# Later V copies for pairs 4 to 7, and K, Q and V loads ahead of FFN weights, in a fused attention and FFN kernel

## The chip, the cores and the metric

The kernel runs on one core of one Trainium2 chip, in one launch. The metric is the device time in microseconds, as the median of several runs; lower is better. A profile is one execution, recorded instruction by instruction, with times counted from the start of its span. The engines are TensorE (PE, with its weight loads as PEld), VectorE (DVE), ScalarE (ACT), GpSimd (POOL) and SyncE (SP); POOL and SP also issue DMAs.

## The reference

Attention with pooled queries over 8 batches of 8 heads, 1152 positions of 64 features, and then a multiplicative FFN on the 4608 rows that come out:

```python
q_pool = q.reshape(B, H, S // 2, 2, D).mean(axis=3)       # 1152 -> 576 queries
scores = 1/sqrt(D) * q_pool @ k.transpose(0, 1, 3, 2)
attn = softmax(scores)
x = (attn @ v).transpose(0, 2, 1, 3).reshape(B * 576, 512)
a = x @ w1;  b = x @ w2                                   # 512 -> 1024
out = ((a * b) @ w3) @ w_out                              # 1024 -> 1024 -> 512
```

Inputs and output are float32; the kernel computes in float16 with float32 accumulation.

## The kernel before

**Pairs.** Two heads form a pair; there are 32 pairs (`NP`), each with 9 key blocks of 128 by 576 queries, 5184 score columns. Scores of consecutive pairs are strung together and cut into chunks of 512 columns. `scores(c)` computes a chunk for both heads on TensorE (line 292) into a PSUM buffer "psc", of which there are three; `expo(c)` takes the exponential on ScalarE into the ring `er` (line 302). `attend` (line 317) multiplies 128 queries by 128 keys of `er` with V; 45 such matmuls make one head, 90 a pair. They accumulate in "po", a single PSUM buffer, so the first matmul of a head waits until `normalize` of the head before (lines 330 and 334, VectorE) has read it.

**Steps.** The main loop has 108 steps (`it`, counted from 0) of three chunks. Each step emits its scores and exponentials, then preparation of later pairs, then a number of PV matmuls from the table `PVS`, around one or two groups of other TensorE work. A group "F" uses the single PSUM buffer "ff", a group "X" one of the three "psc". Groups are, early on, transposes of w3 (line 383) and products T = w3 w_out (line 395), then the FFN's first products "pa" and "pb" (line 411) and its rows "pp" (line 429). Each group's result is copied out by VectorE. With `brief`, where the next group is a transpose, 8 of the step's PV matmuls are emitted ahead of it. Every engine runs its instructions in the order in which they are emitted. After the loop a tail runs the rest of the FFN. In the profile step 12's scores start at 41.97 us, step 13's at 44.67, step 14's at 53.07, step 27's at 94.15, step 28's at 97.25.

**Preparation.** Pairs 1 to 7 are pooled and staged by VectorE (`prep_stage`, lines 122 and 165), transposed by TensorE (`prep_groups`, lines 257 and 169) and copied to `qT` and `kT` by VectorE (lines 263, 264 and 271). From pair 8 on two pairs at a time go another way (`prep_dma`): POOL pools q (line 122) and stages keys (line 142), SP's transposing DMAs make kT and qT (lines 145 and 148), and `settled` (line 152) makes POOL wait for kT before it issues the loads of two later pairs (`load_two`). SP's queue also carries the transposing DMAs of finished outputs (lines 342 and 345) and the stores of the result (line 450).

**V.** A load on POOL's queue brings V of a pair, cast to float16, into one of four staging buffers (`vst`, line 96). `copy_v` (line 135) copies it on VectorE into one of four buffers `vts[P % 4]`, which carry the column for the sum of the softmax. In the loop, `copied` counts these copies. Copies of pairs 1 to 3 are emitted at the end of a step, behind everything else; copies from pair 4 on after the step's scores and preparation, ahead of its PV matmuls and groups: pair 4's in step 12, 5's in step 15, 6's in 19, 7's in 22, 8's in 24. Pair 4 is first used by PV in step 17, pair 5 in 19, pair 6 in 24, pair 7 in 27.

**Loads.** All loads but three at the start go through POOL's queue in the order of emission. `more_loads` adds to it after staging: n = 2 in step 1, n = 3 in step 4, n = 4 in step 8, n = 5 (nothing) in step 11. `load_ffn(h)` loads half of the columns of w1 and w2, 512 KB written each (line 363). Pairs 8 and 9 are loaded by `load` in steps 16 and 19.

Of the kernel before, what the change touches and what calls it, by code (L numbers as in the profile page):

```python
# [23 lines left out]
def kernel(  # L24
# [18 lines left out]
    NP = B * H // 2  # L43
    SCL = 16.0
    NPE = 8
# [31 lines left out]
    def load_q(P):  # L77
        b, h0 = P // 4, 2 * (P % 4)
        if P % 2 == 0 or P == 1:
            qst[P // 2] = stage.tile([128, 2, 18, D], FP16, tag="qst", bufs=2, name="qst")  # L80
        o = 64 * (P % 2)
        nc.gpsimd.dma_start(
            out=qst[P // 2][o:o + 64].rearrange("p u t d -> p u (t d)"),
            in_=q[b, h0:h0 + 2].rearrange("u (p t) d -> p u (t d)", t=18))

    def load_k(P):
        b, h0 = P // 4, 2 * (P % 4)
        kst[P] = stage.tile([128, 2, NJ, D], FP16, tag="kst", name="kst")
        nc.gpsimd.dma_start(  # L89
            out=kst[P].rearrange("p u j d -> p u (j d)"),  # L90
            in_=k[b, h0:h0 + 2].rearrange("u (p j) d -> p u (j d)", j=NJ))

    def load_v(P):
        b, h0 = P // 4, 2 * (P % 4)
        vst[P] = stage.tile([128, 2, NJ, D], FP16, tag="vst", name="vst")
        nc.gpsimd.dma_start(  # L96
            out=vst[P].rearrange("p u j d -> p u (j d)"),
            in_=v[b, h0:h0 + 2].rearrange("u (p j) d -> p u (j d)", j=NJ))

    def load(P):  # L100
        if P < NP:
            load_k(P)
            load_q(P)
            load_v(P)

    def load_two(P):
        load_q(P)
        load_q(P + 1)
        load_v(P)
        load_v(P + 1)  # L110
        load_k(P)
        load_k(P + 1)
# [21 lines left out]
    def copy_v(P):  # L134
        nc.vector.tensor_copy(out=vts[P % 4][:, :, :, 0:D], in_=vst.pop(P))
# [15 lines left out]
    def settled(P):  # L151
        nc.gpsimd.tensor_copy(out=seen, in_=kT[P][0:1, 0, 0:1])
# [9 lines left out]
    def prep_stage(P):  # L162

        pool_q(P)
        nc.vector.tensor_copy(out=new_kc(P).rearrange("p j u d -> p u j d"), in_=kst.pop(P))
# [24 lines left out]
    def spin(n):  # L190
        t = psum.tile([128, 512], FP32, tag="ff", bufs=1, name="spin")
        for _ in range(n):
            nc.tensor.matmul(t[:, 0:128], hot, hot, start=True, stop=True)
# [55 lines left out]
    def prep_groups(P):  # L249

        pp, o = P // 2, 64 * (P % 2)
        new_kq(P)

        def few(t, n):
            if n == 0:
                for c in range(NJ):
                    nc.tensor.transpose(t[:, 128 + 64 * c:192 + 64 * c],
                                        qps[pp][o:o + 64, c].rearrange("p u d -> p (u d)"),
                                        ident[o:o + 64, o:o + 64])
                keys(P, t, range(8, 9))  # L260

        def few_end(t):
            nc.vector.tensor_copy(out=qT[P], in_=t[:, 128:704].rearrange("p (c f) -> p c f", f=64))
            nc.vector.tensor_copy(out=kT[P][:, 8], in_=t[:, 0:128])

        def many(t, n):
            if n == 0:
                keys(P, t, range(0, 8))

        def many_end(t):  # L270
            nc.vector.tensor_copy(out=kT[P][:, 0:8].rearrange("p j f -> p (j f)"), in_=t)  # L271
            del kcs[P]

        return [("t2", FP16, 1, few, few_end), ("t1", FP16, 1, many, many_end)]
# [5 lines left out]
    def scores(c):  # L280
        t = psum.tile([128, 2, CH], FP32, tag="psc", bufs=3, name="psc")
        psc[c] = t
        g = c * CH
        while g < (c + 1) * CH:
            J = g // SQ
            P, j = divmod(J, NJ)
            f0 = g - J * SQ
            ln = min(SQ - f0, (c + 1) * CH - g)
            o = g - c * CH
            for u in range(2):  # L290
                s = slice(64 * u, 64 * u + 64)
                nc.tensor.matmul(t[:, u, o:o + ln].rearrange("p (c f) -> p c f", f=64), kT[P][s, j, :],  # L292
                                 qT[P][s, f0 // 64:(f0 + ln) // 64], start=True, stop=True)
            g += ln

    def expo(c):
        r = (c * CH) % RING
        g = (c - RING // CH + 1) * CH
        if g > 0:
            Pg, Jg = divmod((g - 1) // SQ, NJ)  # L300
            assert nb >= 90 * Pg + 45 + 5 * Jg + 5
        nc.scalar.activation(out=er[:, :, r:r + CH], in_=psc.pop(c), func=AF.Exp,  # L302
                             bias=0.0, scale=SCALE)
# [18 lines left out]
    def ready(n, chunks):  # L322
        P, m = divmod(n, 90)
        j, i = divmod(m % 45, 5)
        return (P * NJ + j) * SQ + min(128 * i + 128, SQ) <= chunks * CH
# [26 lines left out]
    def load_w3(c0, n):  # L352
        if c0 % 4 == 0:
            w3h.append(ffp.tile([128, 4, dff], FP16, tag="g", name="w3h"))
        o = c0 % 4
        nc.gpsimd.dma_start(  # L356
            out=w3h[c0 // 4][:, o:o + n],
            in_=moe_w3.rearrange("(c p) f -> p c f", p=128)[:, c0:c0 + n])

    def load_ffn(h):  # L360
        cols = slice(512 * h, 512 * h + 512)
        for dst, src in ((w1sb, moe_w1), (w2sb, moe_w2)):
            nc.gpsimd.dma_start(
                out=dst[:, :, cols],
                in_=src.rearrange("(c p) f -> p c f", p=128)[:, :, cols])
# [124 lines left out]
    loaded, staged, prepped, copied = 8, 1, 1, 1  # L490

    def more_loads(n):
        if n == 2:
            load_k(4)
            load_q(4)
            load_v(3)
            load_w3(4, 2)
            load_w3(6, 2)
            load_k(5)
            load_q(5)  # L500
            load_v(4)
            load_ffn(0)
        elif n == 3:
            load_k(6)
            load_q(6)
            load_v(5)
            load_ffn(1)
            load_v(6)
        elif n == 4:
            load(7)  # L510
    rest = prep_first()

    n_units = NT // 512
# [37 lines left out]
    def first_it(P):  # L551
        return P * PAIR // (CH * BURST)
# [21 lines left out]
    for it in range(NIT):  # L574
        at = it * BURST * CH / PAIR
        while early and it >= early[0][0]:
            queue.append(early.pop(0)[1])
        while next_unit < EARLY:
            last_b = (512 * (next_unit + 1) - 1) // SQ
            if it < 3 or reached[it - 2] < 360 * (last_b + 1):  # L580
                break
            gens.append(ffn_groups(next_unit))
            next_unit += 1
        for w in range(BURST):
            if it == 0 and w == 2:
                rest()
            if it in (1, 2):
                spin(4)
            scores(BURST * it + w)
            expo(BURST * it + w)  # L590
        if 5 <= staged < NPE and it >= first_it(staged) - 3:
            prep_stage(staged)
            staged += 1
        while 8 <= loaded < NPE + 2 and at >= loaded - 3.4:
            load(loaded)
            loaded += 1
        urgent = False
        if prepped < NPE:
            if it >= first_it(prepped) - (1 if prepped < 5 else 2):
                queue[0:0] = prep_groups(prepped)  # L600
                prepped += 1
                urgent = True
        elif prepped < NP and at >= prepped - 1.95:
            prep_dma(prepped)
            if loaded < NP:
                settled(prepped)
                load_two(loaded)
                loaded += 2
            prepped += 2
        if 4 <= copied < NP and at >= copied - (1.1 if copied >= NPE else 0.6):  # L610
            copy_v(copied)
            copied += 1
        n = PVS[it]
        left = 45 - nb % 45
        brief = bool(queue) and queue[0][2] == 1
        a = left if left < n else 8 if brief and it > 8 and 8 < n < 40 and 8 < left else 0
        assert nb + n <= NPV and ready(nb + n - 1, BURST * it)
        pv(a)
        if head():
            group("F")  # L620
        if head() and (n < 40 or urgent or it < 17):
            group("X")
        pv(n - a)
        if staged < 5 and it >= first_it(staged) - 2:
            prep_stage(staged)
            staged += 1
            more_loads(staged)
        if copied < 4 and at >= copied + 0.25:
            copy_v(copied)
            copied += 1  # L630
        reached.append(nb)
# [43 lines left out]
```

## Time and profile before

| | us |
|---|---|
| median of 5 runs | 424.78 (422.96 to 425.67) |
| profiled execution, its own time | 422.75 |
| its span, first to last instruction | 421.0 |
| TensorE busy | 406.9 (97%) |
| ScalarE busy | 326.8 (78%), nearly all exponentials of 1028 ns |
| VectorE busy | 198.6 (47%) |
| mean granted TensorE clock | 0.996 |
| V copies (line 135) | 32, median 452 ns |
| loads of V, K and Q | 288 KB written each, 8.9, 11.0 and 6.2 us from issue to landing (medians) |

A line of the timeline reads: start in us, length in us, engine, line of the kernel, operation, what it writes and reads, shapes, how many instructions were merged, and in brackets the idle time of the engine just before and what ended it. "PEclk" is the granted clock of TensorE in tenths of full speed. "DMA to landing" counts from the issue of a transfer to its arrival. A busy TensorE is not the same as one at its peak, since the ends of matmuls are modelled.

### The profile page before, as it was taken

How to read it: one execution, taken by the hardware profiler on the slowest of the kernel's cores; microseconds unless marked ns; L12 is line 12 of the kernel's file. 1: busy time of each engine (PE TensorE's matmuls, PEld its weight loads, DVE VectorE, ACT ScalarE, POOL GpSimd, SP SyncE). 2: the span in 40 equal slices, each digit the busy share in tenths (PEclk: the TensorE clock that was granted, in tenths of full speed). 3: DMA queues.
4: the chain of work that ended last, by engine and by line, in shares of the span. 5: the costliest groups of instructions: out<-in, count | busy, mean ns of one | idle time of the engine just before them, and what ended most of it. 6: DMA issues, size and time to landing. Idle time of an engine off the chain costs nothing.

```text
span 421.0 us, 12708 instructions
## 1 busy us (share of the span) xinstructions
PE 406.9 (97%) x5507; PEld 271.7 (65%) x5507; DVE 198.6 (47%) x407; ACT 326.8 (78%) x357; POOL 121.1 (29%) x161
## 2 busy tenths in 40 slices
PE   7899699999999999999999999999999999999996
PEld 5677477766685668665775686667765876544443
DVE  2446546454555553555445534545445444613140
ACT  5999589989888889989888889898888889133332
POOL 6443331343434343434261523234151000000000
PEclk9999899999999999999999999999999999999999
DMA  8999999498989899999999979979997131050404
GB/s 193 202 196 206 199 203 192 79 161 144 167 164 193 120 176 172 205 133 177 176 200 137 145 131 173 168 116 191 171 167 135 44 76 30 14 115 2 100 2 100
DMA packets 95801, 59.76 MB, mean 142 GB/s; under 512 B 65152, under 2 KB 86144, under 8 KB 95744
## 3 DMA queue, kind: packets, MB, share of 16 engines
q0 software_dynamic: 26928, 32.97, 49.2%
q1 hardware_dynamic: 68656, 25.84, 34.8%
q8 instruction: 43, 0.70, 0.7%
q10 hardware_dynamic: 160, 0.13, 0.1%
q14 instruction: 14, 0.11, 0.1%
HBM read 67.11 MB, written 9.44 MB: 182 GB/s over the span
## 4 chain that ended last, share of the span: by engine, by line
PE 84%; DMA 10%; ACT 2%; POOL 1%; issue 1%; DVE 0%; SPq 0%; ACTq 0%
PE po L317 19%; PE psc L292 18%; PE pa L411 15%; PE pb L411 15%; PE pp L429 15%; DMA vst<-in_v_dram 4%; DMA w3h<-in_moe_w_dram 3%; DMA kst<-in_k_dram 3%; PE pT L395 2%; ACT er L302 2%; DMA out_dram<-osb 1%; DMA er<-in_k_dram 1%; PE w3t L383 0%; POOL xT L371 0%; POOL w3h L356 0%
## 5 line engine op out<-in xcount | busy, mean ns | idle before, releaser
L302 ACT ACTIVATE er<-psc 128x1024 f16<-128x1024 f32 x324 | 307.4, 1028 | 44.7 <-PE psc L292 44.6
L317 PEld LDWEIGHTS <-er 128*128 128x128 f16 x2880 | 103.6, 97 | 22.7 <-issue 5.9
L317 PE MATMUL po<-vt,er 128*128 128x65 f16 x2880 | 110.9, 193 | 0.1
L292 PE MATMUL psc<-qT,kT 64*128 64x512 f16 (+7 forms) x1152 | 95.2, 286 | 6.8 <-DVE kT L271 3.6
L423 DVE TENSOR_TENSOR gT<-pb,asb 128x512 f16<-128x512 f32 x72 | 49.8, 692 | 56.0 <-PE pb L411 55.3
L411 PE MATMUL pa<-xT,w1sb 128*128 128x512 f16 x288 | 74.2, 380 | 0.0
L411 PE MATMUL pb<-xT,w2sb 128*128 128x512 f16 x288 | 74.1, 380 | 0.0
L429 PE MATMUL pp<-T,gT 128*128 128x256 f16 (+1 forms) x488 | 67.9, 292 | 0.0
L292 PEld LDWEIGHTS <-kT 64*128 64x128 f16 x1152 | 45.5, 94 | 30.4 <-issue 6.9
L421 DVE COPY asb<-pa 128x512 f32<-128x512 f32 x56 | 38.7, 692 | 40.5 <-PE pa L411 39.4
L429 PEld LDWEIGHTS <-gT 128*128 128x128 f16 x488 | 45.6, 98 | 18.5 <-issue 3.7
L411 PEld LDWEIGHTS <-w2sb 128*128 128x128 f16 x288 | 26.4, 98 | 32.7 <-issue 3.9
L411 PEld LDWEIGHTS <-w1sb 128*128 128x128 f16 x288 | 25.1, 98 | 30.1 <-issue 6.0
L122 POOL TENSOR_TENSOR qp<-qst 128x1152 f16<-128x1152 f16 x12 | 28.3, 2356 | 44.2 <-DMA qst<-in_q_dram 34.1
L441 DVE TENSOR_SCALAR osb<-pp 128x256 f32<-128x256 f32 x49 | 20.8, 425 | 36.8 <-PE pp L429 30.5
L330 DVE RECIPROCAL rz<-po 128x5 f32<-128x5 f32 x64 | 12.4, 194 | 48.1 <-PE po L317 47.7
L334 DVE TENSOR_TENSOR xn<-po,rz 128x320 f16<-128x320 f32 x64 | 31.5, 492 | 2.5 <-DVE rz L330 0.3
L142 POOL COPY kc<-kst 128x576 int32<-128x576 int32 x24 | 16.0, 669 | 48.2 <-DMA kst<-in_k_dram 48.2
L96 POOL DMA_DIRECT2D vst<-in_v_dram x32 | 23.4, 737 | 13.7 <-DMA w3h<-in_moe_w_dram 5.7
L438 ACT ACTIVATE osb<-pp 128x512 f32<-128x512 f32 (+1 forms) x12 | 7.0, 579 | 24.0 <-PE pp L429 20.4
L89 POOL DMA_DIRECT2D kst<-in_k_dram x31 | 22.4, 731 | 7.0 <-DVE rz L330 2.0
L419 ACT COPY asb<-pa 128x512 f32<-128x512 f32 x16 | 9.4, 587 | 16.5 <-PE pa L411 16.5
(42 smaller groups left out, 152.3 us busy)
## 6 DMA issues: line engine op xcount, KB each, us to landing
vst<-in_v_dram POOLq DMA_DIRECT2D x32, 288.0 KB, 8.9
out_dram<-osb SPq DMA_DIRECT2D x70, 128.0 KB, 2.4
kst<-in_k_dram POOLq DMA_DIRECT2D x31, 288.0 KB, 11.0
qst<-in_q_dram POOLq DMA_DIRECT2D x31, 288.0 KB, 6.2
w3h<-in_moe_w_dram POOLq DMA_DIRECT2D x3, 512.0 KB, 14.6
xT<-in_moe_w_out_dram POOLq DMA_DIRECT2D x4, 256.0 KB, 10.7
w1sb<-in_moe_w_dram POOLq DMA_DIRECT2D x2, 512.0 KB, 14.9
w2sb<-in_moe_w_dram POOLq DMA_DIRECT2D x2, 512.0 KB, 16.1
```

What stands on the lines that cost most here:

```text
L89: nc.gpsimd.dma_start(out=kst[P].rearrange("p u j d -> p u (j d)"), in_=k[b, h0:h0 + 2].rearrange("u (p j) d -> p u (j d)", j=NJ))
L96: nc.gpsimd.dma_start(out=vst[P].rearrange("p u j d -> p u (j d)"), in_=v[b, h0:h0 + 2].rearrange("u (p j) d -> p u (j d)", j=NJ))
L122: eng.tensor_tensor(out=qps[pp][r].rearrange("p c u d -> p u c d"), in0=src[:, :, :, 0, :], in1=src[:, :, :, 1, :], op=ALU.add)
L292: nc.tensor.matmul(t[:, u, o:o + ln].rearrange("p (c f) -> p c f", f=64), kT[P][s, j, :], qT[P][s, f0 // 64:(f0 + ln) // 64], start=True, ...
L302: nc.scalar.activation(out=er[:, :, r:r + CH], in_=psc.pop(c), func=AF.Exp, bias=0.0, scale=SCALE)
L317: nc.tensor.matmul(po[P, u][:, VW * x:VW * x + D + 1], er[:, u, r:r + 128], vts[P % 4][:, u, j, 0:D + 1], start=(m == 0), stop=(m == 44), ...
L334: nc.vector.tensor_tensor(out=xn[:, P % 2, :, u, :], in0=acc[:, :, 0:D], in1=rz.to_broadcast([128, 5, D]), op=ALU.mult)
L411: nc.tensor.matmul(p, w[:, mc, ft * 128:ft * 128 + 128], xT[:, mc, t0:t0 + 512], start=(mc == 0), stop=(mc == NC - 1))
L421: nc.vector.tensor_copy(out=asb[ft], in_=p)
L423: nc.vector.tensor_mul(out=gT[:, ft, :], in0=p, in1=asb.pop(ft))
L429: nc.tensor.matmul(p[:, 0:n], gT[:, ft, 128 * i:128 * i + 128], T16[:, ft, n * s:n * s + n], start=(ft == 0), stop=(ft == NF - 1))
L441: nc.vector.tensor_scalar_mul(out=osb, in0=p[:, 0:n], scalar1=1.0 / (SCL * SCL))
```

## The change

Four things differ.

- The V copies of pairs 4 to 7 are emitted at the end of a step: pair 4's in step 15 (was 12), 5's in step 17 (was 15), 6's in step 21 (was 19), 7's in step 24 (was 22). Pair 8's copy, still ahead of its step's PV matmuls, comes in step 25 (was 24), since it waits for its turn behind pair 7's. Later copies stay where they are.
- POOL's load queue behind v4 (V of pair 4) was: ffn(0), k6, q6, v5, ffn(1), v6, k7, q7, v7. It is now: k6, q6, v5, ffn(0), k7, q7, v6, ffn(1), v7. Loads of pairs 8 and later follow as before.
- The loads of pair 7 are emitted one by one instead of by `load(7)`.
- The `brief` split is left out where a step starts exactly at the start of a head (`left` is 45). On TensorE this changes two steps, 13 and 19: the first 8 PV matmuls of the head move behind the w3 transposes and the T product that they stood ahead of.

No instruction is added or removed on any engine.

```diff
@@ more_loads
             load_k(5)
             load_q(5)
             load_v(4)
-            load_ffn(0)
         elif n == 3:
             load_k(6)
             load_q(6)
             load_v(5)
+            load_ffn(0)
+        elif n == 4:
+            load_k(7)
+            load_q(7)
+            load_v(6)
             load_ffn(1)
-            load_v(6)
-        elif n == 4:
-            load(7)
+            load_v(7)
@@ the main loop
-        if 4 <= copied < NP and at >= copied - (1.1 if copied >= NPE else 0.6):
+        if NPE <= copied < NP and at >= copied - 1.1:
             copy_v(copied)
             copied += 1
         n = PVS[it]
         left = 45 - nb % 45
         brief = bool(queue) and queue[0][2] == 1
-        a = left if left < n else 8 if brief and it > 8 and 8 < n < 40 and 8 < left else 0
+        a = left if left < n else 8 if brief and it > 8 and 8 < n < 40 and 8 < left < 45 else 0
...
-        if copied < 4 and at >= copied + 0.25:
+        if copied < NPE and at >= copied + (0.25 if copied < 5 else 0):
             copy_v(copied)
             copied += 1
```

Here `at` is the step's place counted in pairs (it x 1536 / 5184), and `NPE` is 8.

## The prediction

> **What bounds the kernel now.** I began with the page's busy shares and clock row: they say which engine the end hangs on.
>
> ```profile
> span 421.0 us, 12708 instructions
> ...
> PE 406.9 (97%) x5507; PEld 271.7 (65%) x5507; DVE 198.6 (47%) x407; ACT 326.8 (78%) x357; POOL 121.1 (29%) x161
> ...
> PEclk9999899999999999999999999999999999999999
> ```
>
> TensorE is the bound: 97% busy, and from 80 us to the tail its stretches are full (30.00 of 30.00 us in 90 to 120, 80.00 of 80.00 in 120 to 200). So a pause of TensorE removed early is worth its length at the end, unless a later wait takes it back. The one slice with a reduced clock is the fifth, 42 to 53 us. So I asked for the waits between 36 and 60 us (total, times, longest):
>
> ```profile
> ACT er L302 <- PE psc L292: 7.0, 6, 3.4
> DVE vt L135 <- DMA vst<-in_v_dram: 4.9, 2, 4.0
> ...
> PE psc L292 <- DVE kT L271: 3.5, 1, 3.5
> ```
>
> VectorE waits 4.0 us for a V load, TensorE 3.5 us for a copy of keys by VectorE, ScalarE 3.4 us for scores. The timeline of 42 to 53 us (start, us) shows that this is one event:
>
> ```profile
> 43.07 0.43 PE L257 MATMUL t<-ident,qp 64*128 64x64 f16 x9
> ...
> 45.36 0.28 PE L292 MATMUL psc<-qT,kT 64*128 64x256 f16 x2 [0.29 <-ACT er L302]
> ...
> 47.49 0.46 DVE L135 COPY vt<-vst 128x1152 f16<-128x1152 f16 x1 [4.00 <-DMA vst<-in_v_dram]
> 47.87 0.45 DVE L263 COPY qT<-t 128x576 f16<-128x576 f16 x1
> ...
> 48.37 0.68 DVE L271 COPY kT<-t 128x1024 f16<-128x1024 f16 x1
> ...
> 49.10 0.82 PE L292 MATMUL psc<-qT,kT 64*128 64x256 f16 x6 [3.46 <-DVE kT L271]
> ...
> 49.60 1.94 ACT L302 ACTIVATE er<-psc 128x1024 f16<-128x1024 f32 x2 [3.37 <-PE psc L292]
> ```
>
> The copy of V of pair 4 (step 12) stands on VectorE ahead of the copies of qT and kT of pair 4. TensorE had those transposes done by 44.1, but VectorE stood until 47.49, and the scores of pair 4 (in step 13) until 49.10. Then the clock, by windows (columns end in granted clock, DMA share, GB/s):
>
> ```profile
> 48.50:49.00 0.50, 0.00 (x0) 0.00 (x0) 0.50 (x2) 0.00 (x0) 0.20 (x1) 0.84 1.28 211
> ...
> 50.00:51.00 1.00, 1.00 (x15) 1.00 (x14) 0.92 (x2) 1.00 (x2) 0.70 (x1) 0.50 1.23 205
> ...
> 52.00:52.50 0.50, 0.50 (x5) 0.42 (x4) 0.06 (x1) 0.00 (x0) 0.00 (x0) 0.75 1.24 213
> ```
>
> After the pause the clock is half, from about 48.85 to 52.25 us.
>
> **Part 1: the V copy of pair 4 moves behind step 15's work.** What goes: 3.46 us of idle TensorE, and the half clock. TensorE works 49.10 to 52.25, 3.15 us at half rate, so up to 1.57 us lost. By rows: weight transposes and the first product after them take 50.29 to 52.55, 2.26 us, against 57.02 to 58.35, 1.33 us, for the same 16 at full clock; 0.93 lost there, and with the six score matmuls and eight PV matmuls before them, and those after, 1.2 to 1.6. I take 1.5. Sum 3.46 + 1.5 = 5.0 us (4.6 to 5.3).
>
> Can ScalarE follow? It is the tighter engine in this stretch (10.00 of 10.00 us in 10 to 20). Its last exponential before the pause ends at 46.22; before its next long run at 53.57 it idles 3.37 + 2.03 = 5.40 us, so it can give up 5.0. Built forward: L263 at about 43.7, kT copied by 44.9, scores of step 13 done at 45.9, the two groups to 47.2, 22 PV matmuls to 48.0; step 14's first exponential starts near 48.3 instead of 53.57. ScalarE bounds steps 13 to 15, and the gain is 5.2 by its row, 5.0 by TensorE's; I keep 5.0.
>
> What is late next? On VectorE, step 13's pooling of q of pair 5 follows at 45.5 and now meets its load: q5 was issued at 29.09 and took 17.2 us, so 46.3. A new wait of 0.8 us. Queued behind it are the key copy, w3T and T16 copies (0.45 + 0.69 + 0.42 us), done near 48.4. Who waits: the third score chunk of step 14, which takes the PSUM buffer of the T16 copy and is wanted at 48.5; and the transposes of pair 5, not wanted before 49.1. Hidden; if q5 were a microsecond later, up to 1 us of step 14 would show.
>
> The copy itself (0.45 us) runs at the end of step 15, near 54.3, with v4 landed since 47.5 (32.56 + 14.9); pair 4's PV starts in step 17, at 64.23 before, 59 now. Hidden by 4 us.
>
> **Part 2: V copies of 5, 6, 7, and of 8 one step later.** Each is 0.45 us. Copy 5 goes behind step 17's normalisation, into 0.46 us that VectorE sits idle before L263 at 66.82; 6 and 7 behind steps 21 and 24, where the idle is 1 us or more; 8 follows 7 in step 25 and just fits (copies would end 89.3 on the old clock, next item 89.39). Uses come two to four steps later. The 0.87 us that copy 5 waited for v5 at 57.51 also goes; no TensorE wait hung on it. Worth 0, from -0.3 to +0.2. The staging slots come free later (v8 needs copy 4, v9 copy 5, v11 copy 7), but POOL issues v8 at 60.49, v9 at 66.44 and v11 after 90.98, so always after the new copy times (54.8, 61.7, 83.7).
>
> **Part 3: the split of 8 PV matmuls at a head's start.** It alters TensorE's order in two steps, 13 and 19: two groups run before the head instead of behind 8 matmuls of it. In 19 the second group's PSUM buffer comes free at 70.52 and is now asked for at 70.29: 0.25 us idle, against ScalarE bounding the next scores (they waited until 72.41). 0, worst +0.25.
>
> **Part 4: load order.** POOL issues each load when the eighth before it has landed (w1sb's second half at 45.21, k5 landing 27.95 + 17.0 = 44.95), and its queue is full until 67 us. k6, q6, v5 pass ffn(0), four transfers of 512 KB written at some 2.5 us per transfer, so two of them, 5 us earlier; k7, q7, v6 pass ffn(1). FFN weights come later by 4 to 5 us, to about 56 and 65; first uses are 82.9 and 95, now 5 earlier. No cost. Up to q9 the set of transfers is the same, so q9 lands when it did: 64.41 + 14.6 = 79.0.
>
> **Where the gain is cut.** Pairs from 8 on are prepared by POOL and transposing DMAs. Lines of POOL's, SP's and TensorE's timelines and one of the DMA issues (issue to landing, 85 to 87 us):
>
> ```profile
> 79.23 2.35 POOL L122 TENSOR_TENSOR qp<-qst 128x1152 f16<-128x1152 f16 x1 [12.08 <-DMA qst<-in_q_dram]
> ...
> 89.24 0.18 POOL L152 COPY seen<-kT 1x1 f16<-1x1 f16 x1 [6.44 <-DMA kT<-kc]
> ```
>
> ```profile
> 85.53 1.40 SPq L148 DMA_TRANSPOSE qT<-qp  x1
> ```
>
> ```profile
> qT<-qp SPq DMA_TRANSPOSE x1, 4.7
> ```
>
> ```profile
> 94.15 0.83 PE L292 MATMUL psc<-qT,kT 64*128 64x512 f16 x10
> ```
>
> POOL had stood 12 us for q9; so this chain runs on the load stream's time and does not move with TensorE. qT of pair 8 lands at 85.53 + 4.7 = 90.2, and step 27, all of it pair 8, starts at 94.15: slack 3.9 us. With 5.0 gained it would start at 89.15 and waits 1.1 us. What remains is 3.9.
>
> A rule speaks against even that: the SP transposes of finished pairs 2 and 3, issued from 63.3 us, move 5 us forward, into the load stream. By row, they land by 64.53 + 11.0 = 75.5, already before q9. The Trainium skill, "DMA: Bandwidth & Descriptors", section "Issuing engines are not separate DMA queues", says that DMAs from all issuers run on the same 16 engines and interleave. By row and rule together they take the same time from the stream, only sooner: q9 stays at 79.0. By the rule taken alone as a fresh cost (q9 1 to 2 us later) the gain would be 2 to 3.
>
> And the new pause: would it halve the clock? By the row, 3.46 us idle did; pauses of 0.45 to 0.5 us (56.47, 78.33) left it at 1.00; one of 1.1 us the trace doesn't show. The Trainium skill, "TensorE: Matmul & The Clock Gate", section "What's actually happening", puts the fall after an idle window of some 3.4 us. I follow it: no fall, gain 3.9. If it fell, 1.5 more is lost: gain 2.4.
>
> The next pair, 10: qT lands 105.72 + 3.4 = 109.1, wanted near 113.9; 4.8 of slack, enough for 3.9. Pair 12 has 8.
>
> **Sum.** 421.0 - 5.0 + 1.1 = 417.1 of span; the profiled run's own time was 422.75, so 1.75 around it, 418.85. The median is 424.78, 2.0 above that run; 424.78 - 3.9 = **420.9 us**.
>
> **Rivals.** (a) The whole gain stays: pair 8 is ready by 89.1, because q9 lands 1.1 us sooner. 424.78 - 5.0 = 419.8. For it: a DMA stream whose landings vary; against: the full queue. (b) A larger wait at pair 8, or a clock that falls there, or q5 showing: 422.4 (gain 2.4, 1.3 to 3.4). (c) The change does not do what it says: VectorE's wait goes over to another load, q5, before the keys are copied. The order on VectorE speaks against it (pair 5's pooling stands behind pair 4's copies). Gain 47.5 - 46.3 = 1.2, within the noise: 423.6. (d) Slower: q9 lands late. The place is step 27, the price: each microsecond takes one, and from 2.3 late the pause passes 3.4 us and costs the half clock too, so at 2.4 nothing is left, and from 3.7 it is slower by over 0.3%; at 4, 3.9 - 4 - 1.5 = -1.6, 426.4. For it: pair 8's slack rests on one transfer 14.6 us in flight; against: nothing new is ahead of q9.
>
> **Chances.** Forecast 0.62 (own range 420.0 to 422.0), (a) 0.14, (b) 0.12, (c) 0.06, (d) 0.06. 0.3%, 1.3 us, is what a measurement of this kernel tells from no change. Faster 0.88, same 0.06, slower 0.06. The range goes from (a) with its 5.3 and scatter, 419.2, to the weak end of (b), 423.4, and leaves out some 0.17.
>
> **What would show it.** No VectorE wait for a V load at 43 to 48 us and clock 1.00 throughout 42 to 53; step 14's scores near 48.0; a wait of VectorE on q5 of 0.8 at 45 to 46; POOL's pooling again at 79 and kT settled at 89; TensorE idle about 1.1 us before step 27's scores near 90.2, waiting for qT. Wrong if q9 lands elsewhere than 78 to 80, or if steps 13 to 26 lose time that the old trace doesn't show.

## The result, and the profile after

The changed kernel takes 422.06 us (median of 25 runs, 417.82 to 425.82), the kernel before 423.73 in the same comparison (44 runs, 422.32 to 426.08). The ratio is 0.9932, with a 95% interval from 0.9914 to 0.995: faster, by some 2.9 us, where 3.9 were forecast. The ratio leaves out the three longest of the 25 runs (424.49 to 425.82) as slow, though two of them have a granted clock (0.994 and 0.995) that runs it keeps have too; with them the medians are 1.7 us apart and the means 2.4. The profiled execution took 418.47 us, with a span of 416.7; the forecast for it was 418.85 and 417.1. So this one run kept nearly all of the gain, and most others did not: 5 of the 25 are below 419 us. The single runs now spread over 8 us, those of before over 4.

The page of the profile after: span, busy shares, granted clock.

```profile
span 416.7 us, 12709 instructions
...
PE 406.1 (97%) x5507; PEld 271.1 (65%) x5507; DVE 200.2 (48%) x407; ACT 326.7 (78%) x357; POOL 121.0 (29%) x161
...
PEclk9999999999999999999999999999999999999999
```

The reduced slice at 42 to 53 us is gone. The timeline of that stretch, of the kernel after (start, us, and in brackets the idle time before):

```profile
45.90 0.61 PE L292 MATMUL psc<-qT,kT 64*128 64x256 f16 x8 [0.29 <-ACT er L302]
...
46.63 0.76 DVE L122 TENSOR_TENSOR qp<-qst 64x1152 f16<-64x1152 f16 x1 [0.58 <-DMA qst<-in_q_dram]
...
48.53 0.83 PE L292 MATMUL psc<-qT,kT 64*128 64x384 f16 x10
49.03 4.69 ACT L302 ACTIVATE er<-psc 128x1024 f16<-128x1024 f32 x5 [0.44 <-PE psc L292]
```

TensorE runs through step 13's scores without the 3.46 us pause. VectorE has a wait of 0.58 us for q5 in place of the 4.00 us for v4, and no one waits for it. Step 14's scores start at 48.53 instead of 53.07, though this run's step 12 had started 0.53 us later (42.50 against 41.97): the stretch is 5.1 us shorter. From step 15 to step 99 every third step starts 4.5 to 4.6 us ahead of the run before the change; nothing is given back until 0.3 us near step 102; qT of pair 30 landed at 333.2, when step 101 had begun at 332.8, which fits.

The chain of POOL and the transposing DMAs, in the same run: POOL's timeline, TensorE's, and the landing of qT of pair 8 (issued at 84.75).

```profile
78.34 2.36 POOL L122 TENSOR_TENSOR qp<-qst 128x1152 f16<-128x1152 f16 x1 [10.42 <-DMA qst<-in_q_dram]
...
86.75 0.18 POOL L152 COPY seen<-kT 1x1 f16<-1x1 f16 x1 [4.83 <-DMA kT<-kc]
```

```profile
89.60 0.82 PE L292 MATMUL psc<-qT,kT 64*128 64x512 f16 x10
```

```profile
qT<-qp SPq DMA_TRANSPOSE x1, 3.4
```

q9 came 0.9 us sooner than before, kT of pair 8 took 4.7 us from issue instead of 6.3, and qT 3.4 instead of 4.7: it landed at 88.2, and step 27 began at 89.60 without a wait. The forecast pause of 1.1 us at this place is not there.

### The profile page after: what moved, and what is told of

Same layout as the page of the kernel before. It is cut to its first block, busy times and chain, and to the rows that moved or that the text cites. A ratio compares the mean times of both kernels' runs of the same rounds, so it can differ in the third digit from the quotient of the medians.

```text
span 416.7 us, 12709 instructions
## 1 busy us (share of the span) xinstructions
PE 406.1 (97%) x5507; PEld 271.1 (65%) x5507; DVE 200.2 (48%) x407; ACT 326.7 (78%) x357; POOL 121.0 (29%) x161
## 4 chain that ended last, share of the span: by engine, by line
DMA 68%; PE 18%; POOL 9%; issue 2%; SPq 1%; POOLq 0%; ACT 0%; DVE 0%
DMA kst<-in_k_dram 35%; DMA kT<-kc 14%; DMA vst<-in_v_dram 7%; DMA qst<-in_q_dram 7%; PE pa L411 5%; PE pp L429 5%; PE pb L411 5%; DMA w3h<-in_moe_w_dram 3%; POOL qst L82 3%; POOL vst L96 2%; POOL kc L142 2%; PE po L317 2%; PE psc L292 1%; DMA qT<-qp 1%; POOL kst L89 1%
```

## The experiments

There are twelve measurements, in three groups of four: ten other kernels, one of them twice, and the changed kernel once more. In each group all shared one chip and the runs of the kernel before. Two questions were put: which part of the change makes the gain, and where the longer runs lose it again.

### The V copies alone

```diff
 # from the kernel before
-        if 4 <= copied < NP and at >= copied - (1.1 if copied >= NPE else 0.6):
+        if NPE <= copied < NP and at >= copied - 1.1:
...
-        if copied < 4 and at >= copied + 0.25:
+        if copied < NPE and at >= copied + (0.25 if copied < 5 else 0):
```

> Only the V copies of pairs 4 to 7 (and with them 8) are moved; load order and the split of PV matmuls are those of before. Theory A (the gain is the removed wait for v4 on VectorE; the load order adds nothing to it): the same as the full change, ratio to before near 0.993, no VectorE wait for v4 at 43 to 48 us, TensorE clock 1.00 there, v4 still landing near 47.5. Theory B (the copies can only be late without harm because k6 to v7 come sooner): a new wait for a K, Q or V load in steps 13 to 24, and at most 1 us gained.

Measured: 422.57 us (15 runs, 418.45 to 426.65), ratio 0.9935 (0.991 to 0.9961); as with the full change, and the medians are 1.4 us apart. Its step 15 started 4.5 us ahead of the kernel before, and step 18 4.8. So the later copies make the gain, and the median shows no need of the load order or of the split of PV matmuls.

One wait of theory B is there all the same (VectorE's timeline, then TensorE's):

```profile
69.72 0.76 DVE L122 TENSOR_TENSOR qp<-qst 64x1152 f16<-64x1152 f16 x1 [2.46 <-DMA qst<-in_q_dram]
...
71.95 0.40 PE L292 MATMUL psc<-qT,kT 64*128 64x128 f16 x4 [1.11 <-DVE w3T L388]
```

VectorE waits 2.46 us for q of pair 7, and the w3T copy behind it keeps a PSUM buffer from the scores: TensorE's lead falls from 4.8 us at step 18 to 3.9 at step 24. In the old load order q7 landed at 69.7 us here and at 67.7 in the run before, where VectorE came to it later. In the new order it landed at 61.6 (changed kernel), and no such wait is left. So the load order guards part of the gain, 0.9 us in this run, too little to show in the medians.

The profiled run, 423.30 us, was one of the longer ones, and shows what they lose (TensorE's timeline, and below it a window: from:to, length, busy us of PE, PEld, DVE, ACT and POOL with the number of instructions, granted clock, DMA share, GB/s):

```profile
291.21 0.34 PE L292 MATMUL psc<-qT,kT 64*128 64x384 f16 x2 [3.07 <-DMA qT<-qp]
```

```profile
292.00:294.00 2.00, 2.00 (x28) 1.78 (x28) 1.36 (x4) 0.67 (x1) 2.00 (x4) 1.00 0.77 113
```

TensorE waits 3.07 us for qT of pair 26, deep in the attention loop, and 0.6 us in all for qT of pairs 18 and 30. Its lead, 3.0 us at step 87, is gone at step 90.

### The load order alone

```diff
 # from the changed kernel: copies and split as before
-        if NPE <= copied < NP and at >= copied - 1.1:
+        if 4 <= copied < NP and at >= copied - (1.1 if copied >= NPE else 0.6):
...
-        if copied < NPE and at >= copied + (0.25 if copied < 5 else 0):
+        if copied < 4 and at >= copied + 0.25:
```

> Only the load order of the change; copies and split as before. Theory A: v4 is ahead of all the reordered loads, so the 4 us wait of VectorE, the 3.5 us of TensorE and the half clock stay: within 0.3% of before (423.7). Theory B: part of the gain is here, 1 us or more below before.

Measured: 423.37 us (22 runs), ratio 0.9982 (0.9967 to 0.9997): at most 0.3%, 0.8 us by the ratio. The waits of this kernel (total, times, longest) still hold the event:

```profile
DVE vt L135 <- DMA vst<-in_v_dram: 5.2, 1, 5.2
...
PE psc L292 <- DVE kT L271: 4.8, 2, 4.6
```

One V wait is left of the two before, that of v4; v5's is gone. With v5 sooner in the new order, copy 5 has no wait even where it stood. The gain of the whole change is not in the loads.

### The changed kernel once more

> The changed kernel once more beside the others: ratio 0.993, with single runs from 418 to 425. Theory C (in its longer runs pair 8 starts late, since its q load or transposes land later than step 27 wants them): if its profile is of a longer run, TensorE idles before step 27 or 33 for a wait on qT or kT. Theory D (the scatter comes from all over): no such wait, steps longer everywhere.

Measured: 422.51 us (19 runs, 418.50 to 424.59), ratio 0.9962 (0.9942 to 0.9981). The profiled run was again a longer one, 423.28 us (TensorE's timeline, and a window as above):

```profile
201.57 0.50 PE L292 MATMUL psc<-qT,kT 64*128 64x384 f16 x2 [2.57 <-DMA qT<-qp]
202.00 0.73 PE L317 MATMUL po<-vt,er 128*128 128x65 f16 x10
202.54 3.10 PE L429 MATMUL pp<-T,gT 128*128 128x256 f16 x16
```

```profile
202.00:204.00 2.00, 2.00 (x19) 1.58 (x18) 0.69 (x2) 1.02 (x1) 1.10 (x2) 0.50 1.10 206
```

This run was 4.9 us ahead of the kernel before at step 30, 4.4 at step 36, after a 0.33 us wait for qT of pair 10, 3.8 at step 60, after VectorE's normalisation had waited 1.23 us for a transposing DMA of finished outputs, and 0.6 us behind at step 63: a pause of 2.57 us for qT of pair 18, and half the clock after it. So theory C is right that a late qT takes the gain back, but wrong on the place: pair 8 was in time here too. The lead of the chain over TensorE, pair by pair (kT landed, as POOL's copy on line 152 shows it, and the start of the first step that uses the pair, us):

| pair | before | after, 418.47 us | copies alone, 423.30 us | after again, 423.28 us |
|---|---|---|---|---|
| 8 | 89.2, 94.2 | 86.8, 89.6 | 87.2, 90.2 | 86.2, 89.2 |
| 10 | 107.7, 113.3 | 106.2, 108.8 | 106.8, 109.4 | 108.5, 108.4 |
| 18 | 192.2, 202.1 | 192.6, 197.5 | 197.9, 198.2 | 198.5, 198.3 |
| 26 | 281.3, 290.5 | 282.4, 286.0 | 289.8, 287.5 | 285.1, 291.1 |

(qT lands behind kT; pair 10, 18 and 26 are wanted in the third chunk of their step, some 0.6 us after its start.) Before, TensorE came so late that the chain had 5 to 10 us in hand at these pairs. Now it has 2 to 5 in a good run. TensorE takes 22.1 us for a round of two pairs where it has no wait (step 27 to 101 in the run before, 94.2 to 337.3). The chain took 21.1 us a round in the run before (POOL's first pooling of q to its last, 79.2 to 311.2 in 11 rounds), but 21.6, 22.0 and 21.6 in the three runs of the changed copies. So lead comes back at no more than 0.1 to 1 us a round, and rounds differ by several us: pair 26's kT landed at 282.4, 289.8 and 285.1 in these three.

Why did the pause of 2.57 us halve the clock, and the longer one of 3.07 not? The clock's records in the traces answer it. In all fourteen profiles every change of the granted clock lies a whole number of times 3.41 us after its first rise (in the run before it rises at 4.46 and changes at 48.84 and 52.25, 13 and 14 times 3.41 later). So I cut each run into such stretches and took TensorE's idle time in each. The stretches around the pause of the copies alone (first two lines, of its profile) and ahead of the fall of this run (third line):

```profile
286.37:289.78 3.41, 1.78 (x38) 1.32 (x36) 0.42 (x1) 2.52 (x3) 0.00 (x0) 1.00 1.07 205
289.78:293.19 3.41, 1.98 (x25) 1.70 (x26) 1.00 (x3) 1.16 (x2) 3.11 (x6) 1.00 0.88 115
```

```profile
198.17:201.58 3.41, 0.84 (x18) 0.45 (x14) 0.00 (x0) 1.94 (x2) 2.79 (x5) 1.00 1.30 124
```

The longer pause fell across a border: 1.63 us idle on one side, 1.44 on the other. The shorter one lay in one stretch, which was idle for 2.57 us. Over the fourteen profiles, all 21 stretches at full clock with 1.88 us idle or more were followed by half clock, and none of the 1665 with 1.63 or less. At half clock, a stretch with at most 0.27 us idle ended it, and one with 0.69 or more did not. So what counts in these runs is the idle time within one stretch, and where a pause falls decides what it costs. These are counts over traces; no kernel was made to move a pause across a border.

This was taken as theory E: the upstream gain of some 5 us is always there, and single runs lose what the chain's rounds take. It rests on two profiles of longer runs; the next kernels test it.

### The second half of w1 and w2 behind pair 9

```diff
 # from the changed kernel
             load_v(6)
-            load_ffn(1)
             load_v(7)
...
             load(loaded)
             loaded += 1
+            if loaded == 10:
+                load_ffn(1)
```

> The changed kernel with the second half of w1 and w2 loaded behind pair 9's loads instead of ahead of v7. Its first use is step 28. Theory C: q9 lands some 5 us sooner (near 73 instead of 78), kT of pair 8 is there near 82, 7 us ahead of step 27, so every run keeps the whole upstream gain: median near 418.5, runs within 2 us. Theory D: median and scatter as in the changed kernel, 421 to 422 and 418 to 425.

> The kernel with the second half of w1 and w2 behind pair 9's loads once more, for its scatter. Theory E: it gives the chain 2 us of lead at pair 8, so most but not all runs keep the gain: median 419 to 420. If the five runs of its first time were luck: median 421.5 to 422.5, as the changed kernel.

Measured: 419.11 us in five runs, ratio 0.9866 (0.9838 to 0.9893), and 418.15 in six on another chip, ratio 0.9898 (0.9858 to 0.9937). Of these 11 runs 9 are between 417.47 and 420.29 and two at 423.4 and 423.7. The time is as expected, the road less so. q of pair 8 was pooled at 76.3 us in the first profile and 75.0 in the second, where 73 was expected for q9; kT of pair 8 landed at 86.6, taking 6.6 us, and at 83.4, taking 4.5, where 82 was expected. Neither of the two profiles has a wait for qT: at pair 8 it landed 3.9 and 4.6 us before its step, against 1.4 in the changed kernel's first profile. Some 2 us of that come from TensorE, which is only 2.7 and 2.5 us ahead of the kernel before in these two profiles (both of runs above their median), and not 4.6.

### No wait on kT ahead of the loads

```diff
 # from the changed kernel
                 prep_dma(prepped)
                 if loaded < NP:
-                    settled(prepped)
                     load_two(loaded)
```

> The changed kernel without the wait of POOL on kT ahead of the loads of two later pairs (line 152); it carries no data. Theory E (the V wait's 4.5 to 5 us are always gained, and what single runs lose again is lost where the POOL and DMA chain of pairs 8 to 31, about 21 us for two pairs against the 22 that TensorE takes, comes late at one pair, as at pair 18 and pair 26 in the two profiles of longer runs): the loads start some 5 us sooner in each round of the chain, qT is there well ahead of its step, no TensorE wait on qT; median near 418.5, runs within 2 us. Rival F (the chain is bound by the DMA engines, so that transposes only take longer next to the loads): the chain's round stays at 21 us, kT takes 8 to 10 us instead of 4.8, median 421 to 423 as in the changed kernel or longer.

Measured: 433.11 us (6 runs, 431.43 to 436.96), ratio 1.0235 (1.0195 to 1.0274). Rival F, and more than it said. The landing of the transposes (median over 12, us from issue) in this kernel, and then in the changed kernel:

```profile
kT<-kc SPq DMA_TRANSPOSE x12, 11.0
qT<-qp SPq DMA_TRANSPOSE x12, 11.0
```

```profile
kT<-kc SPq DMA_TRANSPOSE x12, 4.7
qT<-qp SPq DMA_TRANSPOSE x12, 3.4
```

Next to the loads the transposes take two to three times as long. All that TensorE lost to qT here was one pause of 9.8 us at pair 8, whose kT took 16.0 us; the half clock around it took 2.3 us more. From pair 10 on there was no wait for qT, and the chain's round was 20.7 us (21.6 in the changed kernel): what the wait on line 152 buys is not a quicker round, but the pair that TensorE wants next.

### v4 ahead of k5 and q5

```diff
 # from the kernel before
+            load_v(4)
             load_k(5)
             load_q(5)
-            load_v(4)
```

> The kernel before, with only the load of v4 put ahead of k5 and q5; copies where they were. v4 lands near 45 instead of 47.5, k5 and q5 1.5 us later each, q5 near 47.5. Theory A (the arrival of v4 under the copy that stands ahead of pair 4's key copies is the whole cause): VectorE waits 1 to 1.5 us for v4, TensorE's pause falls to under 1.5 us and the clock stays at full rate, so about 3.5 to 4.5 us are gained upstream; in the median, less what theory E takes back, 421 to 422. Rival (c) of the prediction (the wait goes over to q5): VectorE waits over 1.5 us on q5 and TensorE idles for it at step 14; nothing gained.

Measured: 425.02 us (22 runs), ratio 1.0027 (1.0014 to 1.004): slightly slower than before, where 421 to 422 was expected. Copy 5 on VectorE before the change, for comparison:

```profile
57.51 0.46 DVE L135 COPY vt<-vst 128x1152 f16<-128x1152 f16 x1 [0.87 <-DMA vst<-in_v_dram]
```

VectorE's timeline, and then TensorE's, of this kernel:

```profile
44.05 0.46 DVE L135 COPY vt<-vst 128x1152 f16<-128x1152 f16 x1 [0.40 <-DMA vst<-in_v_dram]
...
58.27 0.58 DVE L135 COPY vt<-vst 128x1152 f16<-128x1152 f16 x1 [5.19 <-DMA vst<-in_v_dram]
```

```profile
59.83 0.61 PE L292 MATMUL psc<-qT,kT 64*128 64x320 f16 x4 [3.97 <-DVE w3T L388]
60.37 3.60 PE L395 MATMUL pT<-xT,w3T 128*128 128x256 f16 x16
```

With v4 in time, TensorE has no pause at step 13, and step 15 starts 3.6 us ahead. Then pair 5's copy, still ahead of its step's groups, meets v5. Before the change this copy waited 0.87 us, since VectorE itself was late; with the first wait gone it waits 5.19, and the w3T copy behind it holds a PSUM buffer that the scores want. TensorE pauses 3.97 us, runs at half clock, and from step 18 on is 3.1 us behind. q5, at 47.5, cost VectorE 1.29 us and TensorE 0.98 at step 14. So the arrival of v4 under the early copy was the whole cause of the first pause, but removing it for one copy only hands the wait to the next.

### Fewer loads in the chain

```diff
 # from the changed kernel; V of pairs 10 to 31 is left out
     def load_v(P):
+        if P >= 10:
+            return
...
     def copy_v(P):
+        if P >= 10:
+            return
```

> The changed kernel with V of pairs 10 to 31 neither loaded nor copied (those pairs use V of pairs 6 to 9), which takes a third off the chain's loads and some 22 copies of 0.45 us off VectorE. Theory E: the chain's round falls below 20 us, qT is always early, no TensorE wait on qT: median near 418, runs within 2 us. If the longer runs come from elsewhere (theory D): median and scatter as in the changed kernel.

Measured: 419.26 us (6 runs, 418.60 to 419.89), ratio 0.99 (0.9878 to 0.9922). PV of pairs 10 to 31 then uses V of pairs 6 to 9. All runs lie within 1.3 us, no wait for qT, and the profiled run is 4.6 us ahead of the kernel before from step 15 to step 107. The chain's round is 20.5 us, where under 20 was expected, and the median is 1 us over the expected 418. With a third of the chain's loads away the longer runs are gone, which fits the spread coming from the chain. VectorE is also rid of 22 copies of 0.45 us here, and no run takes away the loads alone.

### A late q9

```diff
 # from the changed kernel
         while 8 <= loaded < NPE + 2 and at >= loaded - 3.4:
+            if loaded == 8:
+                load_ffn(0)
             load(loaded)
```

> The changed kernel with the first half of w1 and w2 loaded a second time (the same bytes to the same place, 1 MB written) ahead of pair 8's loads, so that q9 lands some 5 us later. Theory E (pair 8's slack in the changed kernel is under 1 us, and each microsecond of the chain there costs TensorE one): qT of pair 8 lands near 93.5 instead of 88.7, TensorE waits some 4 us at step 27 and runs at half clock after it, 5 us lost there: median 425 to 428, slower than before. Theory D: no wait at step 27, median 421 to 423.

Measured: 427.04 us (22 runs, 423.60 to 432.29), ratio 1.0058 (1.0034 to 1.0083). q was pooled at 84.0 instead of 78.3. TensorE's timeline:

```profile
94.19 1.47 PE L292 MATMUL psc<-qT,kT 64*128 64x512 f16 x10 [4.65 <-DMA qT<-qp]
95.59 1.89 PE L411 MATMUL pa<-xT,w1sb 128*128 128x512 f16 x4
```

The pause and the half clock behind it (four "pa" matmuls in 1.89 us instead of 1.04) turn a lead of 4.7 us at step 24 into 2.5 us of lag at step 30. By step 102 the lag is 3.9 us, with two more waits for qT. This is rival (d) of the prediction brought about: with q9 5.7 us late the change is slower than no change.

### Later FFN weights without the later copies

```diff
 # from the kernel before
             load_v(5)
-            load_ffn(1)
             load_v(6)
...
             load(loaded)
             loaded += 1
+            if loaded == 10:
+                load_ffn(1)
```

> The kernel before, with only the second half of w1 and w2 moved behind pair 9's loads, its V copies where they were. Theory E with A: the wait for v4 at 43 to 47 us stays and sets the time, since the chain has slack already: 423 to 424.5. If loading w1 and w2 later were the gain of the better kernel by itself: 420 or less.

Measured: 424.34 us (14 runs), ratio 0.9999 (0.9981 to 1.0017). More lead for the chain is worth nothing while the pause at v4 sets the time; with the pause gone it is worth 1 to 4 us (0.987 to 0.990 against 0.993 to 0.996).

### The wait on kT at pair 8 alone

```diff
 # from the kernel with the second half of w1 and w2 last
-                    settled(prepped)
+                    if prepped == 8:
+                        settled(prepped)
```

> The kernel with the second half of w1 and w2 last, and the wait of POOL on kT kept at pair 8 alone. Without that wait anywhere the 9.8 us pause was all at pair 8. Theory E: from pair 10 on the chain has lead enough to bear kT's 11 us, and gains lead by earlier loads: no wait on qT, median 418 to 418.5 and no run at 423. Theory F (next to the loads the transposes come too late here as well): a wait of some us at pair 10 or 12, median 421 or more.

Measured: 434.18 us (6 runs), ratio 1.0193 (1.0154 to 1.0232): theory F. The profiled run, the longest of the six at 439.02 us, has pauses of 9.4 us for qT of pair 10 and 4.3 for that of pair 18. The lead that the chain was to gain did not come; transposes at 10.9 us for kT and 10.1 for qT (medians) cost more than earlier loads bring. The wait on line 152, which looks idle, is what brings the next pair in time.

### V behind q

```diff
 # from the kernel with the second half of w1 and w2 last
             load_v(6)
-            load_v(7)
...
-            load(loaded)
+            load_k(loaded)
+            load_q(loaded)
             loaded += 1
             if loaded == 10:
+                load_v(7)
+                load_v(8)
+                load_v(9)
                 load_ffn(1)
```

> The kernel with the second half of w1 and w2 last, and v7, v8 and v9 behind q9 as well: three transfers of some 1.5 us go behind it, so q9 lands 3 us sooner (near 72 to 73) and kT of pair 8 near 81 to 83. v7 is wanted at 83 by its copy. Theory E: lead at pair 8 of 5 us or more, median 418 or a little below, fewer long runs. If v7 to v9 come late for their copies: VectorE waits in steps 24 to 26, and nothing gained.

Measured: 419.19 us (6 runs, 418.23 to 421.01), ratio 0.9879 (0.985 to 0.9909). q of pair 8 was pooled at 73.6, and kT and qT issued at 77.5 and 82.3; no VectorE wait for v7 to v9. But kT landed only at 85.9, where 81 to 83 was expected: it took 8.5 us, next to the loads that now came behind. qT was there 3.2 us before its step, not the 5 us or more expected. No run is at 423, though with six runs that is not much. This kernel and the one with the second half of w1 and w2 last, which it can't be told from, beat both kernels. What each still pays is the wait named in the prediction, q5 on VectorE (first line) and through it TensorE at step 14 (second; both from the waits of the V-behind-q kernel):

```profile
DVE qp L122 <- DMA qst<-in_q_dram: 2.9, 2, 1.8
...
PE psc L292 <- DVE T L399: 1.0, 1, 1.0
```

## Why the prediction was right, and where it was not

The median, 422.06, lies within the range and just over the forecast's own range (420.0 to 422.0), nearest to the 422.4 of rival (b); the gain by the ratio was 2.9 us for 3.9. That it came so near is in part luck: the forecast set out from 424.78, the median of five runs, where 44 runs gave 423.73. From there the same gain leads to 419.8, and the result is 2.2 us above it.

- **The pause and the clock (part 1), 5.0 us:** right. The stretch from step 12 to step 14 is 5.1 us shorter, at full clock. That the pause was caused by the copy's place was shown from two sides: later copies alone give all of it, v4 sooner removes the same pause. The clock's 1.5 us was read in a run with one stretch of half clock. Two later profiles in which the pause still stands, those of the load order alone and of later FFN weights without the later copies, have two (6.83 us), at mean clocks of 0.992 and 0.990. Of 111 runs of the kernel before in the three groups, 61 have a mean clock of 0.992 or less, and their median is 1.2 us above that of the others (424.5 against 423.3). So the old pause probably cost more in most runs than in the one that was read; this is inferred from the clocks, not profiled.
- **What is late next on VectorE, q5, 0.8 us, hidden:** right, 0.58 measured and hidden. Its warning also held: where q5 came later, in four of the kernels (v4 first, V behind q, and the two runs with the second half of w1 and w2 last), 1.0 to 1.2 us of step 14 showed.
- **Copies 5 to 8 (part 2), worth 0:** the number was right and its ground was not. "No TensorE wait hung on it" was read in a run where the earlier pause had hidden it. With v4 in time and copy 5 left in place, that wait grew from 0.87 to 5.19 us and undid the gain. In the old load order, moving copy 5 as well was necessary. The new order lands v5 at 53.4 us in place of 57.5; no run leaves copy 5 alone in place there.
- **The split (part 3), 0:** not tried by itself; the copies alone, with the old split, gave the same ratio.
- **Load order (part 4), no cost:** right; the FFN weights landed some 6 us later, not 4 to 5, and were still in time. It is of little use by itself (0.9982), but not useless: without it, in one profile, the later copies met q7 (1.11 us of TensorE), a term that the prediction does not have.
- **"Where the gain is cut":** this step failed. It said that 1.1 us is lost at pair 8 and nothing later ("enough for 3.9", "pair 12 has 8"). The chain's dependence on the load stream was right, and its arithmetic gave nearly the right number for the profiled run (4.3 us of span, 3.9 forecast) by two errors that cancelled in part: the pause was 0 and not 1.1, but a later start and step 102 took 0.8. The cause of the smaller median is another, as far as two longer runs show it: slack was read off one execution as though landing times were fixed. They vary by several us, and the chain of pairs 8 to 31 has 11 rounds in which to be late. In the two longer profiled runs most of the loss was at pairs 10, 18 and 26, where I had counted on slack. Once V of pairs 10 to 31 was left out, all six runs kept most of the gain.
- **The clock at a short pause:** I followed the Trainium skill, "TensorE: Matmul & The Clock Gate", section "What's actually happening", which puts the fall after an idle window of some 3.4 us, and took no fall below that. The runs show a fall after 2.57 us (pair 18) and none after 3.07 (pair 26), and a stretch need not be wholly idle: 1.88 us of 3.41 was enough. For 1.1 us the assumption was safe, since no stretch with 1.63 us idle or less was followed by a fall; for the rivals, which let it fall from 3.4 us on, it was not. A fall costs up to 1.7 us (half of 3.41) with one stretch of half clock, and up to 3.4 with two.
- **Rivals:** (a) names what the profiled run did: pair 8's qT landed at 88.2 us, in time, with q9 0.9 us sooner. (b), a larger wait behind the removed one, names what the two longer profiled runs did, at other pairs than it said. (d) was brought about and came out near its price: for q9 5.7 us late its arithmetic gives 3.9 - 5.7 - 1.5 = -3.3, and the median was 3.2 us over that of before (2.5 by the ratio). Its terms fit less well: step 27 waited 4.65 us and the half clock, two stretches long, took 2.6.

## What to carry to other kernels

A pause that is removed early on moves every later deadline forward; list what runs on its own time (here loads and transposes) and ask for the slack at each later meeting, over several executions and not one. Where a chain of transfers is hardly faster than the engine it feeds (21.1 to 22.0 against 22.1 us a round), give it lead in the same change: here weights that weren't needed yet could go behind it. And when a wait in an in-order queue is removed, look at the next instruction of its kind: its short wait may be short only because of the first, as with copy 5 and q7 here.

## What was not expected of the hardware

- A transposing DMA beside loads took 11.0 us where it took 4.7 (kT) and 3.4 (qT) with the loads held back; holding POOL's loads until kT had landed was worth some 11 us of the whole (433.11 against 422.51, on two chips), nearly all of it at one pair.
- The granted clock fell to half after a pause of 2.57 us in one run, and stayed at 1.00 through one of 3.07 us in another. It changed only at borders 3.41 us apart, and fell where 1.88 us or more between two borders had been idle.
- The changed kernel's executions spread over 8 us (25 runs), where the chain of transfers has little lead, and over 1.3 us (6 runs) with V of 22 pairs left out.
